# Attention scores by one plain fp32 product in place of three fp32r products of split parts

## The chip, the cores and the metric

The kernel runs on one core of a Trainium2 chip. Its engines are TensorE (PE; its weight loads are listed as PEld), VectorE (DVE), ScalarE (ACT), GpSimd (POOL) and SyncE (SP), which issues most DMAs. Each engine works through its own queue in order and waits on semaphores for the others. The metric is the device time of one execution in microseconds, as the median of several.

## The reference

Sliding-window attention with four sink keys, then two mixture-of-experts layers. The change concerns the scores alone:

```python
def _attn_ref(q, k, v, n_sink, window) -> np.ndarray:      # q, k, v: 4 x 8 x 768 x 64, fp32
    scale = 1.0 / np.sqrt(D)
    scores = scale * np.matmul(q, k.transpose(0, 1, 3, 2))
    is_sink = pos[None, :] < int(n_sink)                   # n_sink = 4
    in_window = (rel >= 0) & (rel < int(window))           # window = 128
    scores = np.where(is_sink | in_window, scores, -1000000000.0)
    scores = scores - np.max(scores, axis=-1, keepdims=True)
    a = np.exp(scores)
    a = a / (np.sum(a, axis=-1, keepdims=True) + 1e-09)
    return np.matmul(a, v).astype(np.float32)

def reference(**kwargs):
    x = attn_out.transpose(0, 2, 1, 3).reshape(B * S, H * D)
    x = _moe_ref(x=x, **moe_kwargs)      # one expert of 8 per token, by its logits and a bias per modality
    return _moe2_ref(x=x, **moe2_kwargs) # experts with a fixed capacity
```

## The kernel before

**Tiling.** The attention stage works on pairs of heads, 16 in all (4 batches of 4 pairs). The two heads of a pair lie on partitions 0 to 63 and 64 to 127 of `qr` and `kr`, transposed, so that the contraction is over 64 partitions. A pair has six query blocks of 128 rows. The loop runs over the 96 blocks; block i of a pair is scored against 260 columns: 128 keys of the block before, 4 sink keys and its own 128 keys (132 columns for the first block, which has no block before it).

**Order.** The stage is pipelined by hand: `ORDER` (line 174) lists what is issued in each turn of the loop, and each step works on a block some turns back. Per turn: the exponential of the block before (`ex`), loads (`ld`), the score product (`qk`), a piece of background work such as the router's bookkeeping for a finished batch (`bg`), the product with v of six blocks back (`pv`), mask and row maximum of this block (`mm`), transposes of P of two blocks back (`tr`, `se`); every second turn the output rows (`ro`, `oT`, `xo`) and the sink columns (`sp`, `st`, `so`). The scores `sp` have two buffers in PSUM, so block n waits until the exponential of block n-2 has read its own.

**Scores before.** Each load of q and k is split for the pair that follows: `split_hi` rounds to fp32r on ACT (`qh` is q times 0.125, `kh` is k), `split_lo` forms what the rounding left (`ql` on DVE; `kl` on POOL for three pairs in four and on DVE for the fourth), a third of a tile at a time, at six turns per pair. `qk_mm` adds three products for each head: qh kh, qh kl, ql kh. The two heads' products use different partitions and different PSUM banks.

**Sinks.** The four sink columns of P are packed with their own split parts in `psk` (`sinkpack`, POOL), transposed on PE against `identr`, an fp32r copy of the identity (`sinktr`), copied out by ACT, and used in `rows` together with the transposed output. The transposes of P itself (L359), the product with v (L388) and the second part of `rows` (L428) are plain fp32; the sink transposes (L405) and the first part of `rows` (L426) are fp32r.

**After the attention.** `moe1` and `moe2` compute the expert layers by split fp32r products. The ids, rows and weights of the first experts are fetched from within the attention's loop, on SP's and POOL's queues.

Of the kernel before, what the change touches and what calls it, by code (L numbers as in the profile page):

```python
# [10 lines left out]
F32 = mybir.dt.float32  # L11
F32R = mybir.dt.float32r
BF = mybir.dt.bfloat16
I32 = mybir.dt.int32
AF = mybir.ActivationFunctionType
OP = mybir.AluOpType
# [3 lines left out]
B, H, S, D = 4, 8, 768, 64  # L20
NB = S // 128
NP = H // 2
# [6 lines left out]
KW = NB * SEG  # L29
# [33 lines left out]
def bc(ap, shape):  # L63
    return ap.to_broadcast(shape)
# [7 lines left out]
def load_consts(nc, g, cpool, cst):  # L72
    g.cp = cpool
    g.cst = cpool.tile([128, C_W], F32, name="cst")
    g.ident = g.cst[:, C_ID:C_ID + 128]
    g.identr = cpool.tile([128, 128], F32R, name="identr")
    g.tri = cpool.tile([128, 128], BF, name="tri")
    g.ones = cpool.tile([128, 128], BF, name="ones")
    g.iota = g.cst[:, C_IOTA:C_IOTA + 128]
    g.wz = cpool.tile([128, 512], BF, name="wz")  # L80
    nc.gpsimd.memset(g.wz, 0.0)

    def derive():
        nc.vector.tensor_copy(g.identr, g.ident)
        nc.vector.tensor_copy(g.tri, g.cst[:, C_TRI:C_TRI + 128])
        nc.vector.memset(g.ones, 1.0)
    g.cst_load = lambda: nc.sync.dma_start(g.cst, cst)
    g.cst_derive = derive
# [82 lines left out]


LM, LE, LT, LP, LK, LS, LO, LR = 0, 1, 2, 6, 3, 6, 8, 9
ORDER = "ex ld qk ini bg pv mm tr ro oT sp st xo so lo hi se"


def attention(ctx, tc, g, qT, kT, v4, vsT, vsR, wg, put_x, after_batch, bg, drain=True):
    nc = tc.nc
    one = ctx.enter_context(tc.tile_pool(name="at1", bufs=1))
    wk = ctx.enter_context(tc.tile_pool(name="at2", bufs=2))  # L180
# [4 lines left out]
    raw, qk, vt = {}, {}, {}  # L185

    def load_pair(p):
        if p >= B * NP:
            return
        b, pr = divmod(p, NP)  # L190
        qr = wk.tile([128, S], F32, name="qr")
        kr = wk.tile([128, KW], F32, name="kr")
        nc.sync.dma_start(qr, qT[b, pr])
        nc.sync.dma_start(kr, kT[b, pr])
        raw[p] = (qr, kr)

    def split_hi(p, c):
        if p >= B * NP:
            return
        if c == 0:  # L200
            qk[p] = [wk.tile([128, S], F32R, name="qh"), wk.tile([128, S], F32R, name="ql"),
                     wk.tile([128, KW], F32R, name="kh"), wk.tile([128, KW], F32R, name="kl")]
        qr, kr = raw[p]
        qh, ql, kh, kl = qk[p]
        c2 = c % 3
        if c < 3:
            r = slice(256 * c2, 256 * c2 + 256)
            nc.scalar.activation(qh[:, r], qr[:, r], AF.Copy, scale=0.125)
        else:
            r = slice(264 * c2, 264 * c2 + 264)  # L210
            nc.scalar.activation(kh[:, r], kr[:, r], AF.Copy)

    def split_lo(p, c):
        if p >= B * NP:
            return
        qr, kr = raw[p]
        qh, ql, kh, kl = qk[p]
        c2 = c % 3
        if c < 3:
            r = slice(256 * c2, 256 * c2 + 256)  # L220
            nc.vector.scalar_tensor_tensor(ql[:, r], qr[:, r], 0.125, qh[:, r].bitcast(F32), op0=OP.mult,
                                           op1=OP.subtract)
        else:
            r = slice(264 * c2, 264 * c2 + 264)
            (nc.gpsimd if p % 4 < 3 else nc.vector).tensor_tensor(kl[:, r], kr[:, r], kh[:, r].bitcast(F32), op=OP.subtract)

    def load_v(p):
        if p < B * NP:
            vt[p] = wk.tile([128, NB, 2, D], F32, name="vr", bufs=3)
            nc.sync.dma_start(vt[p], v4[p // NP, p % NP])  # L230

    load_pair(0)
    g.cst_load()
    load_pair(1)
    load_v(0)

# [17 lines left out]
    for s in range(2):  # L254
        o = slice(64 * s, 64 * s + 64)
# [7 lines left out]
    nc.gpsimd.memset(bd.bitcast(F32), 0.0)  # L263
    vsh = wk.tile([96, B * NP, 72], F32, name="vsh", bufs=1)
    msk = one.tile([128, 3, 128], I32, name="msk")
    for c in (0, 3, 1, 4, 2, 5):
        split_hi(0, c)
    for c in (0, 3):
        split_lo(0, c)
    for i, c in ((1, C_M0), (2, C_M1), (0, C_CAUS)):  # L270
        nc.vector.tensor_copy(msk[:, i, :], g.cst[:, c:c + 128])

    def init(n):
        V = nc.vector
        if n < 2:
            for c in ((4, 1), (5, 2))[n]:
                split_lo(0, c)
        if n == 0:
            g.cst_derive()
            V.tensor_copy(rw[:, :, 0:128], bc(g.ident[:, None, :], [128, NP, 128]))  # L280
        if n in (2, 4):
            g.pw = ps.tile([96, B * NP, 8], F32, name="px")
        for p in {2: range(4), 4: range(4, 10), 5: range(10, 16)}.get(n, ()):
            nc.tensor.matmul(g.pw[:, p, :], vst[:, p, :], wgp[:, p % NP, :], start=True, stop=True)
        if n in (3, 6):
            r = slice(0, 4) if n == 3 else slice(4, 16)
            V.tensor_copy(vsx[:, r, 64:72], g.pw[:, r])
            V.tensor_copy(vsh[:, r].bitcast(F32R), vsx[:, r])
        if n in (4, 7):
            r = slice(0, 4) if n == 4 else slice(4, 16)  # L290
            V.tensor_tensor(vsh[64:96, r].bitcast(F32R), vsx[64:96, r], vsh[64:96, r], op=OP.subtract)
        k = n - 5 if n < 9 else (4 + (n - 9) // 2 if (n - 9) % 2 == 0 else 16)
        if 0 <= k < 16:
            c, m = divmod(k, 4)
            blk, hd = divmod(m, 2)
            mk = g.cst[:96, C_BD + m:C_BD + m + 1]
            r = slice(4 * c, 4 * c + 4)
            o, i = bd[:, r, blk, 64 * hd:64 * hd + 64], vsh[:, r, 0:64]
            if c > 0:
                nc.gpsimd.tensor_scalar(o, i, mk, None, op0=OP.mult)  # L300
            else:
                nc.scalar.activation(o, i, AF.Copy, scale=mk)
            V.tensor_scalar(bd[:, r, blk, 128 + 8 * hd:136 + 8 * hd], vsh[:, r, 64:72], mk, None, op0=OP.mult)

    st = {}

    def unit(n):
        p, i = divmod(n, NB)
        b, pr = divmod(p, NP)
        return b, pr, p, i  # L310

    def qk_mm(n):
        b, pr, p, i = unit(n)
        qh, ql, kh, kl = qk[p]
        sp = ps.tile([128, 2, 512], F32, name="sp", bufs=2)
        c0 = 128 if i == 0 else 0
        k0 = SEG * i - 128 + c0
        for j, (x, y) in enumerate(((qh, kh), (qh, kl), (ql, kh))):
            for hd in range(2):
                o = 64 * hd  # L320
                nc.tensor.matmul(sp[:, hd, c0:260], x[o:o + 64, 128 * i:128 * i + 128],
                                 y[o:o + 64, k0:k0 + 260 - c0], start=(j == 0), stop=(j == 2))
        st[n] = K()
        st[n].sp = sp

# [75 lines left out]
    def sinktr(gn, pt):  # L401
        s = st[2 * gn + 1]
        s.skp = (ps.tile([128, 512], F32, name="pt") if pt is None else pt)[0:96, 384:512]
        sk = psk[gn % 4]
        nc.tensor.transpose(s.skp.bitcast(F32R), sk.rearrange("p a b c -> p (a b c)"), g.identr)  # L405

    def sinkout(gn):
        s = st[2 * gn + 1]
# [47 lines left out]
    def at(n, lag, last=NU):  # L456
        return n - lag if lag <= n < last + lag else None

    def sink(n, lag):
        m = n - lag  # L460
        return m // 2 if 0 <= m and m % 2 == 0 and m // 2 < NU // 2 else None

    def when(f, *a):
        return lambda n: None if f(n) is None else a[0](f(n))

    def loads(n):
        b, pr, p, i = unit(n)
        if i == 1:
            load_pair(p + 2)
            load_v(p + 1)  # L470

    def one_of(n, f):
        p, i = divmod(n, NB)
        f(p + 1, i)

    ops = dict(
        ld=when(lambda n: at(n, 0), loads),
        qk=when(lambda n: at(n, 0), qk_mm),
        mm=when(lambda n: at(n, LM), mask_max),
        ex=when(lambda n: at(n, LE), exp),  # L480
        tr=when(lambda n: at(n, LT), trans),
        se=when(lambda n: at(n, LT), sel),
        st=when(lambda n: sink(n, LS), lambda k: sinktr(k, st[2 * k + LS - LT].ptt if 2 * k + LS - LT < NU else None)),
        so=when(lambda n: sink(n, LS), sinkout),
        sp=when(lambda n: sink(n, LK), sinkpack),
        oT=when(lambda n: sink(n, LO), outT),
        ro=when(lambda n: sink(n, LR), rows),
        xo=when(lambda n: sink(n, LR), xout),
        pv=when(lambda n: at(n, LP), pv),
        hi=when(lambda n: at(n, 0), lambda n: one_of(n, split_hi)),  # L490
        lo=when(lambda n: at(n, 1), lambda n: one_of(n, split_lo)),
        bg=lambda n: bg.pop(1),
        ini=init)
    for n in range(NU + LR + 3):
        for op in ORDER.split():
            if op == "qk" and n < 6:
# [1446 lines left out]
```

## Time and profile before

| what | value |
|---|---|
| three runs | 942.4, 949.34, 950.2 us (median 949.34) |
| the profiled execution | 948.23 us, span 946.4 us, mean granted clock 0.951 |
| PE busy over the span | 877.8 us (93%) |
| DVE, ACT, POOL busy | 668.4, 429.9, 386.3 us |
| attention stage, by the last of its output rows on PE | to 212 us |

The span is from the first to the last instruction; the execution's own time is 1.8 us longer. Busy shares over the span mix three stages, so the attention is read from its own stretches. Durations of matmuls overlap, so PE's busy time says less than the starts of its rows. The granted clock is TensorE's, as a share of 2.4 GHz; at any one time it is 1.00 or 0.50.

### The profile page before, as it was taken

The numbers are of one execution on the slowest core, as the hardware profiler recorded it, in microseconds if no ns is written. First come the engines' busy times: TensorE is split into PE (matmuls) and PEld (weight loads), VectorE is DVE, ScalarE is ACT, GpSimd is POOL, SyncE is SP. The second block draws the span as 40 slices with busy tenths as digits, with TensorE's granted clock in tenths as the row PEclk, the third lists the DMA queues.
The fourth block names the chain that finished last, engine by engine and source line by source line (L and its number), as shares of the span: only waits on it lengthen the run. The fifth ranks groups of instructions, "written<-read, shape, count | busy, mean of one in ns | idle before, by whom it ended". The sixth has DMA issues, their size and how long they took to land. (4 is left out here: it accounts for less than half of the span.)

```text
span 946.4 us, 15922 instructions
## 1 busy us (share of the span) xinstructions
PE 877.8 (93%) x5226; PEld 697.2 (74%) x5232; DVE 668.4 (71%) x1876; ACT 429.9 (45%) x1231; POOL 386.3 (41%) x636
## 2 busy tenths in 40 slices
PE   8998989998999999999998868889999998999993
PEld 4666767666888888888876635778788787798992
DVE  5999989867669697878863936878878677723210
ACT  4787968764343334343334503233334342345430
POOL 5897969783311010100000003645364554457441
PEclk9899999899999999999996877999999999999997
DMA  8344646366444444433434206234453433434200
GB/s 235 103 145 127 134 138 119 119 229 202 111 157 134 135 146 138 161 129 128 133 114 135 87 15 211 90 123 157 146 180 109 145 123 101 144 124 157 89 34 36
DMA packets 68952, 124.02 MB, mean 131 GB/s; under 512 B 9075, under 2 KB 21365, under 8 KB 68726
## 3 DMA queue, kind: packets, MB, share of 16 engines
q1 hardware_dynamic: 62166, 103.41, 35.3%
q0 software_dynamic: 6688, 19.43, 6.5%
q8 instruction: 46, 0.75, 0.3%
q14 instruction: 52, 0.43, 0.2%
HBM read 103.11 MB, written 19.71 MB: 130 GB/s over the span
## 5 line engine op out<-in xcount | busy, mean ns | idle before, releaser
L965 ACT ACTIVATE hh<-ph 128x384 fp32r<-128x384 f32 (+1 forms) x112 | 60.2, 538 | 272.3 <-PE ph L956 271.8
L956 PE MATMUL ph<-xh,w1h 128*128 128x384 f32 (+1 forms) x448 | 170.9, 382 | 0.0
L899 PE MATMUL y<-w2h,hh 128*128 128x512 f32 x400 | 163.5, 409 | 0.0
L956 PE MATMUL ph<-xh,w1l 128*128 128x384 f32 (+1 forms) x448 | 163.3, 364 | 0.0
L956 PE MATMUL ph<-xl,w1h 128*128 128x384 f32 (+1 forms) x448 | 161.9, 364 | 0.0
L899 PE MATMUL y<-w2h,hl 128*128 128x512 f32 x400 | 159.3, 398 | 0.0
L899 PE MATMUL y<-w2l,hh 128*128 128x512 f32 x400 | 159.0, 398 | 0.0
L966 DVE SCALAR_TENSOR_TENSOR hl<-ph,hh 128x384 fp32r<-128x384 f32 (+1 forms) x112 | 68.5, 611 | 110.2 <-ACT hh L965 109.7
L1111 POOL DMA_INDIRECT xg<-xd,ent x26 | 27.4, 1055 | 219.3 <-DMA ent<-idtab 169.4
L852 POOL TENSOR_TENSOR w2l<-w2r,w2h 128x512 fp32r<-128x512 f32 x64 | 87.7, 1374 | 52.5 <-ACT w2h L848 37.6
L1151 DVE SCALAR_TENSOR_TENSOR junk<-yr,wgb 128x512 f32<-128x512 f32 x160 | 103.3, 684 | 0.0
L956 PEld LDWEIGHTS ph<-xh,w1h 128*128 128x128 f32 x448 | 86.4, 193 | 10.4
L956 PEld LDWEIGHTS ph<-xh,w1l 128*128 128x128 f32 x448 | 86.2, 192 | 9.7
L956 PEld LDWEIGHTS ph<-xl,w1h 128*128 128x128 f32 x448 | 85.5, 191 | 7.8
L899 PEld LDWEIGHTS y<-w2h,hl 128*128 128x128 f32 x400 | 76.2, 191 | 17.1 <-DVE hl L1004 0.4
L899 PEld LDWEIGHTS y<-w2h,hh 128*128 128x128 f32 x400 | 76.6, 192 | 12.4 <-ACT hh L1003 0.4
L899 PEld LDWEIGHTS y<-w2l,hh 128*128 128x128 f32 x400 | 76.4, 191 | 12.2 <-DVE w2l L852 0.3
L871 DVE TENSOR_TENSOR w1l<-w1r,w1h 128x512 fp32r<-128x512 f32 x96 | 73.6, 767 | 13.5 <-ACT w1h L866 13.5
L866 ACT ACTIVATE w1h<-w1r 128x512 fp32r<-128x512 f32 x128 | 79.7, 623 | 5.7 <-DMA w1r<-in_w_dram 3.0
L351 ACT ACTIVATE P<-sp,mx 128x132 f32<-128x132 f32 x192 | 69.3, 368 | 28.4 <-DVE mx L340 27.7
L848 ACT ACTIVATE w2h<-w2r 128x512 fp32r<-128x512 f32 x128 | 79.4, 624 | 2.4 <-issue 2.0
L1596 POOL DMA_INDIRECT xg<-xs,idx x24 | 25.0, 1042 | 111.3 <-DMA w2r<-in_w_dram 90.6
(351 smaller groups left out, 1682.7 us busy)
## 6 DMA issues: line engine op xcount, KB each, us to landing
w1r<-in_w_dram SPq DMA_DIRECT2D x32, 1024.0 KB, 5.4
w2r<-in_w_dram SPq DMA_DIRECT2D x32, 1024.0 KB, 6.0
xs<-yr SPq DMA_DIRECT2D x26, 256.0 KB, 6.1
kr<-in_kT_dram SPq DMA_DIRECT2D x16, 396.0 KB, 3.5
qr<-in_qT_dram SPq DMA_DIRECT2D x16, 384.0 KB, 4.0
vr<-in_v_dram SPq DMA_DIRECT2D x16, 384.0 KB, 4.0
xd<-xb SPq DMA_DIRECT2D x16, 384.0 KB, 4.5
wgb<-in_wg2T_dram SPq DMA_DIRECT2D x1, 2048.0 KB
```

Of the source, the lines that this page charges most:

```text
L351: nc.scalar.activation(s.P[:, i % 2, hd, :], s.sp[:, hd, 128:260], AF.Exp, bias=s.mx[:, hd:hd + 1], accum_out=s.sm[:, i % 2, hd:hd + 1])
L848: nc.scalar.activation(ch[1][c][0], r[:, q, :], AF.Copy)
L852: eng.tensor_tensor(lo, r[:, q, :], h.bitcast(F32), op=OP.subtract)
L866: nc.scalar.activation(h, v, AF.Copy)
L871: eng.tensor_tensor(lo, v, h.bitcast(F32), op=OP.subtract)
L899: nc.tensor.matmul(o, l, r, start=(first and i == 0), stop=(end and i == 2))
L956: nc.tensor.matmul(ph, wp[:, c, :], xp_[:, c, 0:NTK], start=(d == 0 and i == 0), stop=(d == 3 and i == len(cut[d]) - 1))
L965: nc.scalar.activation(hh, ph, AF.Relu)
L966: nc.vector.scalar_tensor_tensor(hl, ph, 0.0, hh.bitcast(F32), op0=OP.max, op1=OP.subtract)
L1111: self.nc.gpsimd.indirect_dma_start(out=self.xg[j][:, a, :], out_offset=None, in_=self.G.xd[0:k, :], in_offset=bass.IndirectOffsetOnAxis(a ...
L1151: V.scalar_tensor_tensor(junk, yr[:, 0:DM], 1.0, wgb[:, e, :], op0=OP.mult, op1=OP.mult, accum_out=lg[:, e:e + 1])
L1596: self.nc.gpsimd.indirect_dma_start(out=xg[:, a, :], out_offset=None, in_=self.xs, in_offset=bass.IndirectOffsetOnAxis(ap=self.idx[k][:, 0 ...
```

## The change

The scores of each head come from one product in plain fp32, of the loaded k and of q times 0.125 (`qs`, made on ACT in three pieces per pair at every second block). `split_hi`, `split_lo` and their four tiles go; `kr` is read by the product itself and gets a third buffer. The sink transposes use the fp32 identity and read `psk` as plain fp32; `identr` goes.

```diff
@@ load_consts
-    g.identr = cpool.tile([128, 128], F32R, name="identr")
-        nc.vector.tensor_copy(g.identr, g.ident)
@@
-ORDER = "ex ld qk ini bg pv mm tr ro oT sp st xo so lo hi se"
+ORDER = "ex ld qk ini bg pv mm tr ro oT sp st xo so sq se"
@@ load_pair
-        kr = wk.tile([128, KW], F32, name="kr")
+        kr = wk.tile([128, KW], F32, name="kr", bufs=3)
@@
-    def split_hi(p, c):
...
-    def split_lo(p, c):
...
+    def scale_q(p, c):
+        if p >= B * NP or c % 2:
             return
         if c == 0:
+            qk[p] = wk.tile([128, S], F32, name="qs")
+        r = slice(128 * c, 128 * c + 256)
+        nc.scalar.activation(qk[p][:, r], raw[p][0][:, r], AF.Copy, scale=0.125)
@@ qk_mm
-        for j, (x, y) in enumerate(((qh, kh), (qh, kl), (ql, kh))):
-            for hd in range(2):
-                o = 64 * hd
-                nc.tensor.matmul(sp[:, hd, c0:260], x[o:o + 64, 128 * i:128 * i + 128],
-                                 y[o:o + 64, k0:k0 + 260 - c0], start=(j == 0), stop=(j == 2))
+        for hd in range(2):
+            o = 64 * hd
+            nc.tensor.matmul(sp[:, hd, c0:260], qs[o:o + 64, 128 * i:128 * i + 128], kr[o:o + 64, k0:k0 + 260 - c0],
+                             start=True, stop=True)
@@ sinktr
-        nc.tensor.transpose(s.skp.bitcast(F32R), sk.rearrange("p a b c -> p (a b c)"), g.identr)
+        nc.tensor.transpose(s.skp, sk.bitcast(F32).rearrange("p a b c -> p (a b c)"), g.ident)
```

On PE, in the steady part of the loop (the first two blocks of a pair) before:

```order
L321 MATMUL sp<-kh,qh 128x132 x2
L321 MATMUL sp<-kl,qh 128x132 x2
L321 MATMUL sp<-kh,ql 128x132 x2
L359 MATMUL pt<-cst,P 128x128 x2
L405 MATMUL pt<-identr,psk_177 96x128
L321 MATMUL sp<-kh,qh 128x260 x2
L321 MATMUL sp<-kl,qh 128x260 x2
L321 MATMUL sp<-kh,ql 128x260 x2
L388 MATMUL po<-lu,vr 64x256 x2
L359 MATMUL pt<-cst,P 128x128 x2
L426 MATMUL px<-bd,skT 128x288
L428 MATMUL px<-rw,oT 128x144 x2
```

The same place on PE after the change, where line 291 is `qk_mm` and 375 `sinktr`:

```order
L291 MATMUL sp<-kr,qs 128x132 x2
L329 MATMUL pt<-cst,P 128x128 x2
L375 MATMUL pt<-cst,psk_176 96x128
L291 MATMUL sp<-kr,qs 128x260 x2
L358 MATMUL po<-lu,vr 64x256 x2
L329 MATMUL pt<-cst,P 128x128 x2
L396 MATMUL px<-bd,skT 128x288
L398 MATMUL px<-rw,oT 128x144 x2
```

Six score products of a block became two; the operations around them stand as they stood.

On DVE, two blocks of a pair before (masks and maxima at L338 and L340, output rows at L442 to L448):

```order
L338 COPY_PREDICATED sp<-msk,sp 128x2x128
L340 TENSOR_REDUCE mx<-sp 128x2
L442 TENSOR_SCALAR rv<-sm 128x4
L443 RECIPROCAL rv<-rv 128x4
L445 TENSOR_TENSOR xb<-px,rv 128x256
L448 TENSOR_TENSOR lp<-px,rv 128x2x16
L221 SCALAR_TENSOR_TENSOR ql<-qr,qh 128x256
L338 COPY_PREDICATED sp<-msk,sp 128x2x128
L340 TENSOR_REDUCE mx<-sp 128x2
L225 TENSOR_TENSOR kl<-kr,kh 128x264
```

The same place on DVE after (the lines are 30 lower):

```order
L308 COPY_PREDICATED sp<-msk,sp 128x2x128
L310 TENSOR_REDUCE mx<-sp 128x2
L412 TENSOR_SCALAR rv<-sm 128x4
L413 RECIPROCAL rv<-rv 128x4
L415 TENSOR_TENSOR xb<-px,rv 128x256
L418 TENSOR_TENSOR lp<-px,rv 128x2x16
L308 COPY_PREDICATED sp<-msk,sp 128x2x128
L310 TENSOR_REDUCE mx<-sp 128x2
```

The splits between one block's maximum and the next block's mask are gone; nothing took their place.

## Rows read from the trace of the kernel before

**Rows 1.** Stretches: length; PE, PEld, DVE, ACT, POOL busy; granted clock; DMA share; GB/s.
```profile
203.80:212.40 8.60, 7.18 (x58) 4.84 (x56) 3.33 (x18) 2.95 (x11) 7.09 (x12) 1.00 1.01 367
100.00:112.50 12.50, 12.50 (x121) 8.93 (x119) 11.36 (x35) 11.20 (x50) 11.76 (x29) 1.00 0.64 129
162.50:175.00 12.50, 10.28 (x72) 7.26 (x72) 11.51 (x47) 7.53 (x33) 9.07 (x25) 0.73 0.59 188
```
**Rows 2.** Waits, 0 to 205 us: total us, times, longest.
```profile
ACT P L351 <- DVE mx L340: 27.7, 43, 2.8
PEld sp L321 <- ACT P L351: 17.9, 29, 2.4
```
**Rows 3.** PE's timeline, 101 to 108 us: start, us to the end, what.
```profile
101.07 0.30 PE L405 MATMUL pt<-identr,psk 128*96 128x128 f32 x1
101.33 0.39 PE L321 MATMUL sp<-kh,qh 64*128 64x260 f32 x2
101.56 0.28 PE L321 MATMUL sp<-kl,qh 64*128 64x260 f32 x2
101.67 0.28 PE L321 MATMUL sp<-kh,ql 64*128 64x260 f32 x2
101.89 0.65 PE L388 MATMUL po<-lu,vr 128*64 128x256 f32 x4
102.47 0.44 PE L359 MATMUL pt<-cst,P 128*128 128x128 f32 x2
...
102.88 0.65 PE L428 MATMUL px<-rw,oT 128*128 128x144 f32 x4
...
107.39 0.33 PE L321 MATMUL sp<-kh,qh 64*128 64x132 f32 x2
...
107.87 0.44 PE L359 MATMUL pt<-cst,P 128*128 128x128 f32 x2
```
**Rows 4.** PE's timeline: score products of first blocks of three pairs.
```profile
37.86 0.33 PE L321 MATMUL sp<-kh,qh 64*128 64x132 f32 x2
...
118.04 0.33 PE L321 MATMUL sp<-kh,qh 64*128 64x132 f32 x2
...
192.73 0.33 PE L321 MATMUL sp<-kh,qh 64*128 64x132 f32 x2
```
**Rows 5.** Groups by form, 0 to 205 us: count, busy us, mean ns, idle before.
```profile
L388 PE MATMUL po<-lu,vr 128*64 128x256 f32 x184 | 30.9, 415 | 0.0
L428 PE MATMUL px<-rw,oT 128*128 128x144 f32 x176 | 30.3, 296 | 0.0
L225 POOL TENSOR_TENSOR kl<-kr,kh 128x264 fp32r<-128x264 f32 x36 | 27.2, 757 | 0.2
...
L221 DVE SCALAR_TENSOR_TENSOR ql<-qr,qh 128x256 fp32r<-128x256 f32 x48 | 24.7, 516 | 4.7 <-ACT qh L208 4.7
...
L211 ACT ACTIVATE kh<-kr 128x264 fp32r<-128x264 f32 x48 | 20.1, 418 | 0.7 <-DMA kr<-in_kT_dram 0.7
...
L225 DVE TENSOR_TENSOR kl<-kr,kh 128x264 fp32r<-128x264 f32 x12 | 6.4, 534 | 0.0
```
**Rows 6.** The timeline of the loads on PE at 101 us, second pair.
```profile
101.44 0.19 PEld L321 LDWEIGHTS sp<-kl,qh 64*128 64x128 f32 x2
```
**Rows 7.** DVE's timeline around 165 us.
```profile
163.48 0.66 DVE L221 SCALAR_TENSOR_TENSOR ql<-qr,qh 128x256 fp32r<-128x256 f32 x1
...
166.71 0.41 DVE L338 COPY_PREDICATED sp<-msk,sp 128x256 f32<-128x256 int32 x1
```
**Rows 8.** PE's timeline, 168 to 174 us, with idle time before and its releaser.
```profile
168.49 0.48 PE L321 MATMUL sp<-kh,qh 64*128 64x132 f32 x2 [2.22 <-ACT P L351]
...
172.82 1.16 PE L428 MATMUL px<-rw,oT 128*128 128x144 f32 x4
```
**Rows 9.** PE's timeline in the first pair.
```profile
13.65 0.82 PE L284 MATMUL px<-wgp,vst 128*96 128x8 f32 x8 [0.66 <-DMA vst<-in_vsT_dram]
```

More of the change, by code (lines that the diff above doesn't have):

```diff
@@ L195, in load_pair @@
         raw[p] = (qr, kr)
-    def split_hi(p, c):
-        if p >= B * NP:
+    def scale_q(p, c):
+        if p >= B * NP or c % 2:
             return
         if c == 0:
[L201 to L211, printed above, removed]
-    def split_lo(p, c):
[L214 to L225, printed above, removed]
+            qk[p] = wk.tile([128, S], F32, name="qs")
+        r = slice(128 * c, 128 * c + 256)
+        nc.scalar.activation(qk[p][:, r], raw[p][0][:, r], AF.Copy, scale=0.125)
     def load_v(p):
@@ L265, in attention @@
     msk = one.tile([128, 3, 128], I32, name="msk")
[L266 to L269, printed above, removed]
+    for c in (0, 2, 4):
+        scale_q(0, c)
     for i, c in ((1, C_M0), (2, C_M1), (0, C_CAUS)):
@@ L274, in init @@
         V = nc.vector
-        if n < 2:
-            for c in ((4, 1), (5, 2))[n]:
-                split_lo(0, c)
         if n == 0:
@@ L313, in qk_mm @@
         b, pr, p, i = unit(n)
-        qh, ql, kh, kl = qk[p]
+        qs, kr = qk[p], raw[p][1]
         sp = ps.tile([128, 2, 512], F32, name="sp", bufs=2)
@@ L489, in attention @@
         pv=when(lambda n: at(n, LP), pv),
-        hi=when(lambda n: at(n, 0), lambda n: one_of(n, split_hi)),
-        lo=when(lambda n: at(n, 1), lambda n: one_of(n, split_lo)),
+        sq=when(lambda n: at(n, 0), lambda n: one_of(n, scale_q)),
         bg=lambda n: bg.pop(1),
```

## The prediction

> **What bounds the kernel now.** The change touches only the attention stage, the first 212 us of 946.4; what follows it is taken as it is. I read the busy time by stretch first [rows 1]. In a quiet stretch (100 to 112.5 us) PE is busy for 12.50 of 12.50 us, but DVE for 11.36, ACT for 11.20 and POOL for 11.76 as well, so four engines are nearly full together. In a bad stretch (162.5 to 175) PE falls to 10.28 and ACT to 7.53 while DVE keeps 11.51: there DVE sets the pace.
>
> Matmul durations overlap, so a PE that is busy all the time need not be the limit. The order of the starts decides. In a quiet pair (six query blocks of one pair of heads) the PE rows follow each other without a hole [rows 3], and the pair takes 118.04 - 107.39 = 10.65 us [rows 3, 4]. That is PE's floor for a pair. The 13 pairs from 37.86 to 192.73 us took 154.87 us [rows 4], 11.91 each; 13 floors are 138.5, so 16.4 us are excess.
>
> The waits say where the excess comes from [rows 2]: PE's score product waits for ACT's exponential (17.9 us at PE's loads in 29 waits), and the exponential for DVE's maximum (27.7 us in 43). Both scores buffers are then in use: the product of a block cannot start until the exponential of the block two before it has read its buffer. The worst case shows it [rows 7, 8]: from 163.48 to 166.71 us DVE does a split of q (0.66) and some bookkeeping of the router before it gets to the next mask, and PE stands for 2.22 us at 168.49. So the stage is PE's floor, plus what DVE's bursts cost on top.
>
> **What the change removes.** The splits: DVE loses 48 of q (24.7 us) and 12 of k (6.4 us), POOL 36 of k (27.2 us), ACT 48 roundings of k (20.1 us) [rows 5]. In the 13 pairs DVE loses 39/48 of 24.7 plus all 6.4, 26.5 us or 2.0 per pair. On PE 6 products per block become 2. None of these times comes off the end as such: in a quiet pair PE's own work hides them, and they only count where PE waits.
>
> **What it adds: the score product.** Before, a block of 260 columns holds PE from 101.33 to 101.89 us, 0.56 us [rows 3]: 0.11 until the second load may start [rows 6], then three products of two heads, the last two starting 0.11 apart (101.56, 101.67), which is 260 columns at one per cycle of 2.4 GHz. The last takes 0.22 to the next operation, 0.11 of streaming and 0.11 of changing over. Both heads run at once: each row of two records is no longer than one.
>
> No row shows a plain fp32 product on 64 of the 128 rows. The nearest are two. The plain fp32 product of L428 appears as twice as many records as the program has instructions, so each runs as two passes; four passes of 144 columns take 0.65 us from first start to last end, one lasts 0.296, so they start (0.65 - 0.30)/3 = 0.118 apart [rows 3, 5]. That is 0.82 ns a column, two cycles. And the plain product with v (L388), two heads on two halves of the columns: four passes of 256 columns from 101.89 take 0.65 in all, while one lasts 0.415 [rows 3, 5]. One after the other they would take 3 x 0.21 + 0.42 = 1.05. So the two heads' passes run side by side there.
>
> I price the new product like that: 0.11 for the first load, two passes of 260 x 0.82 = 0.21, and 0.11 to change over, 0.65 us against 0.56: **+0.09 per block**. The second load hides under the first pass. For the first block of a pair (132 columns) three products take 0.48 (107.39 to 107.87) [rows 3] and are held by their loads; the new one takes 0.11 + 2 x 0.108 + 0.11 = 0.43: -0.05. The ends of the price are 0.43 (two passes and no overhead) and 1.07 (four passes one after the other, 0.11 + 4 x 0.213 + 0.11); I stay with 0.65, since the L388 row shows the same instruction on two heads.
>
> The Trainium skill speaks against the change here: "FP8 and Floating Point Precision", section TensorE Precision Notes, counts true fp32 as four passes through the array. By that the product goes from three column times to four, an estimate of +0.108 per block in place of +0.09, and the trace agrees with it: two records at two cycles a column. With it the sum below would be 1.2 us higher.
>
> **The sink transposes.** The fp32r one streams 128 columns and stands 0.26 us before the next product (101.07 to 101.33) [rows 3]. Plain, I give it two cycles a column: 128 x 0.41 ns = +0.05 each, three per pair. Ends: 0 and +0.11. The identity's copy on DVE disappears, once.
>
> **PE's floor after.** 10.65 + 5 x 0.09 - 0.05 + 3 x 0.05 = **11.20 us a pair**. The floor rises, because PE is the one engine that gets more work.
>
> **What is left of the excess.** DVE's 2.0 us less and PE's 0.55 more give DVE some 2.5 us of slack per pair, where there was next to none. Single splits then no longer reach PE; the bursts of bookkeeping still do in part. In the 163 us case, 0.57 of the 3.2 us of delay was the split; the rest remains, less what DVE is now ahead, so perhaps 1 us of the 2.2. I take a quarter of 16.4, **4 us**, ends 0 and 10.
>
> **Queues.** ACT's scaling of q stands where the rounding stood; three of six places per pair are empty. On SP the loads of k now wait for PE's last product of the pair before, where they waited for ACT and for POOL or DVE; with a third buffer that is over five blocks before the load is issued, so nothing queues behind it. The loads that follow in the queue (v, x out, the first experts' weights) are issued at the same block as before. Cost 0; if a k load stood, v's load and the write of x would stand behind it, and the PE would wait at the first block of a pair.
>
> **Head and tail.** The first two pairs (7.55 to 37.86) are held by masks, waits for loads and warm-up matmuls; for instance PE stands 0.66 us for vst at 13.65 [rows 9], which remains. Twelve DVE splits leave there, of which I count 1 us in the end after PE's +0.09 per block (ends +1 and -4). The last pair and its drain add 0.5: its six products and sink transposes, with no excess to give back.
>
> **The sum.** 13 x 11.20 + 4 = 149.6 against 154.9: -5.3; head -1; tail +0.5: **-5.8 us**. The profiled execution took 948.23 us (span 946.4, 1.8 around it), 1.1 below the median of the three runs. 948.2 - 5.8 = 942.4; I say **942.5**. One per cent is 9.5 us, which is about what a measurement of this kernel can tell from no change (its own three runs lie between 942.4 and 950.2).
>
> **Rivals.**
> *The heads do not pair up (slower).* On 64 rows the passes of the two heads run one after the other. Against: the fp32r products pair up on rows, and plain ones on columns [rows 3]. For: no row shows both together. Price: +0.51 per block, +0.17 per first block, a pair of 13.5 us; 13 x 13.5 = 175.5, +20.6 with no excess left, +2.3 in the last pair, +4 in the head: **975**. It decides as soon as a block's product holds PE for more than about 0.75 us, since then PE's floor passes 11.9 - 0.3. The skill's "TensorEngine Tiling (Array Packing)", Key Properties, says that tiles work independently, which is for pairing; no run here shows it for this operation.
>
> *The clock falls (slower).* At the lower level L428's four passes take 1.16 us for 0.65 [rows 3, 8], 1.8 times. The quiet stretch and the tail from 203.8 to 212.4, which is mostly plain fp32 work with PE at 7.18 of 8.60 us, were granted 1.00 [rows 1]; the fall at 168 came after a stop of 2.2 us. So PE should be granted the full clock at least as often. A quarter of the 13 pairs at the lower level would cost 36 x 0.8 = 29: **971**. Eight more us at that level take the gain away.
>
> *The excess is not DVE's.* If bursts, and not splits, make all of the 16.4 us, 13 x 11.20 + 16.4 = 162: +7.1 and +0.5, less 1 of the head: **955**, PE's longer products with nothing in return.
>
> *All of it goes (faster).* With POOL and ACT lighter too, the excess vanishes and the head gives 4: 145.6 - 154.9 - 4 + 0.5 = -12.8: **935.5**.
>
> **How the numbers follow.** Forecast 0.58 (spread 937 to 951 by the ends of 4 us of excess and of the head), all of it goes 0.18, excess not DVE's 0.10, heads in turn 0.09, clock 0.05. The range 934 to 958 takes in the first three, 0.86. Faster by over 1% (under 938.7): the 0.18 and some 0.05 of the forecast, 0.23. Slower by over 1%: the 0.14 and 0.02 of the third, 0.16. Within: 0.61.
>
> **What would show it.** A quiet pair of 11.2 us, by the starts of the first blocks' products; a block's product of 0.65 us to the next PE operation, its two passes 0.32 apart, each with two records at one time; DVE under 10 us busy per 12.5 us; the wait of the exponential for the maximum well below 27.7 us; POOL waiting more. I am wrong if the records of the two heads start apart, if quiet pairs still take 10.7, or if the 13 pairs keep their excess with DVE idle.

## The result, and the profile after

The kernel after takes **937.22 us** (median of 9 runs, 932.86 to 940.63) against 948.75 for the kernel before beside it (9 runs, 942.40 to 952.48): ratio **0.9877, 95% interval 0.9858 to 0.9895**. The gain is real and over one per cent. The forecast, 942.5 with a range of 934 to 958, had the direction and held the time, but it gave only 0.6% and lay nearer to no change than the result does.

The profiled execution took 933.44 us (span 931.6), 14.8 below that of before. Its stages, by the same landmarks in both traces:

| stage | before, us | after, us | difference |
|---|---|---|---|
| start to the first block of the third pair | 37.86 | 34.82 | -3.0 |
| the 13 pairs after it | 154.87 | 146.84 | -8.0 |
| last pair and drain, to the first transpose of the expert layers | 19.93 | 20.55 | +0.6 |
| attention in all | 212.66 | 202.21 | -10.45 |
| expert layers and the rest (code unchanged) | 733.7 | 729.4 | -4.3 |

The busy time by stretch of the kernel after; columns as in [rows 1]. The first stretch is the whole of the 13 pairs:

```profile
34.82:181.66 146.84, 145.92 (x1123) 90.62 (x1122) 117.81 (x420) 117.83 (x510) 102.34 (x302) 1.00 0.52 139
...
193.40:202.00 8.60, 7.17 (x56) 4.74 (x56) 3.17 (x17) 2.85 (x10) 7.05 (x12) 1.00 1.05 385
100.00:112.50 12.50, 12.50 (x101) 7.68 (x97) 9.21 (x28) 10.36 (x46) 8.58 (x26) 1.00 0.63 129
```

Against the quiet stretch of [rows 1], PE is still busy throughout (12.50), while DVE went from 11.36 to 9.21, ACT from 11.20 to 10.36 and POOL from 11.76 to 8.58. For the 13 pairs the trace of before has these rows: first all of them, then two single pairs:

```profile
37.86:192.73 154.87, 145.58 (x1280) 102.79 (x1280) 141.23 (x469) 125.82 (x549) 127.56 (x326) 0.97 0.49 129
...
131.47:144.64 13.17, 12.70 (x100) 8.92 (x101) 11.88 (x46) 9.90 (x44) 7.74 (x24) 0.87 0.45 104
168.49:182.07 13.58, 13.58 (x99) 9.65 (x99) 11.33 (x41) 10.39 (x45) 7.56 (x23) 0.75 0.29 89
```

DVE gave back 23.4 us in these pairs and POOL 25.2. The granted clock is the second thing to see: 0.97 before, with 0.87 and 0.75 in two of its longest pairs, and 1.00 after. So a part of the old excess may be TensorE's own time at the lower level; the section on the prediction works out how much.

The waits of the kernel after, 0 to 195 us, answer to [rows 2]:

```profile
POOL lu L337 <- ACT t L335: 59.8, 55, 7.7
...
DVE sp L308 <- PE sp L291: 14.9, 30, 0.8
...
ACT P L321 <- DVE mx L310: 8.6, 18, 1.4
```

The exponential's wait for the maximum fell from 27.7 us in 43 to 8.6 in 18, and a new one stands above it: DVE's mask now waits for PE's product, 14.9 us, where it waited 2.0 us before. The direction of waiting has turned: in the 13 pairs PE is busy for 145.92 of 146.84 us, and it is the bound.

PE's own rows in a quiet pair, which answer to [rows 3], and two first blocks, which answer to [rows 4]:

```profile
102.08 0.50 PE L291 MATMUL sp<-kr,qs 64*128 64x132 f32 x4
102.51 0.44 PE L329 MATMUL pt<-cst,P 128*128 128x128 f32 x2
102.78 0.27 PE L375 MATMUL pt<-cst,psk 128*96 128x128 f32 x1
102.98 0.71 PE L291 MATMUL sp<-kr,qs 64*128 64x260 f32 x4
103.62 0.65 PE L358 MATMUL po<-lu,vr 128*64 128x256 f32 x4
...
113.27 0.49 PE L291 MATMUL sp<-kr,qs 64*128 64x132 f32 x4
...
181.66 0.49 PE L291 MATMUL sp<-kr,qs 64*128 64x132 f32 x4
```

Four records a block are two heads of two passes. The block's product holds PE from 102.98 to 103.62, 0.64 us, and the first block's from 102.08 to 102.51, 0.43. The block's two passes start 0.32 us apart, as forecast. This quiet pair takes 113.27 - 102.08 = 11.19 us, the shortest takes 11.17. The 13 pairs hold 146.84 - 13 x 11.17 = 1.6 us over 13 of the shortest, where before they held 16.4.

### The profile page after: what moved, and what is told of

It reads as the page before. It is cut to its first block, busy times and chain, and to the rows that moved or that the text cites. A ratio compares the mean times of both kernels' runs of the same rounds, so it can differ in the third digit from the quotient of the medians.

```text
span 931.6 us, 15380 instructions
## 1 busy us (share of the span) xinstructions
PE 877.2 (94%) x5034; PEld 680.8 (73%) x5040; DVE 637.6 (68%) x1815; ACT 419.8 (45%) x1183; POOL 354.4 (38%) x600
## 5 line engine op out<-in xcount | busy, mean ns | idle before, releaser
L840 POOL TENSOR_TENSOR w1l<-w1r,w1h 128x512 fp32r<-128x512 f32 x32 | 43.8, 1369 | 62.7 <-ACT w1h L835 62.7
```

The source lines that it names most:

```text
L840: eng.tensor_tensor(lo, v, h.bitcast(F32), op=OP.subtract)
```

## The experiments

Each pair time below runs between the first score products of two pairs; "13 pairs" is from the third to the sixteenth. A stage time is from one profiled execution, a ratio from the timed runs beside the kernel before. "The splits" are the 48 of q on DVE, 12 and 36 of k on DVE and POOL, and 48 roundings of k on ACT. The forecasts below call the run with all splits e1 and the one with DVE's e2.

| kernel | 13 pairs, us | quiet pair | attention, us | ratio of the whole, 95% interval |
|---|---|---|---|---|
| before | 154.87 | 10.65 | 212.66 | 1 |
| after | 146.84 | 11.17 | 202.21 | 0.9877 [0.9858, 0.9895] |
| after, profiled again | 146.86 | 11.18 | 202.31 | 0.9882 [0.9825, 0.9940] |
| after + all splits (e1) | 156.40 | 11.17 | 213.41 | 1.0053 [1.0025, 1.0081] |
| after + DVE's splits (e2) | 149.61 | 11.17 | 205.83 | 0.9971 [0.9938, 1.0005] |
| after + ACT's and POOL's | 153.02 | 11.17 | 209.29 | 0.9972 [0.9939, 1.0004] |
| after + POOL's | 148.05 | 11.17 | 204.35 | 0.9903 [0.9867, 0.9939] |
| after + ACT's | 146.84 | 11.17 | 202.49 | 0.9866 [0.9817, 0.9915] |
| before without low parts | 142.47 | 10.67 | 197.53 | 0.9894 [0.9840, 0.9947] |

### Relief or product: all splits kept, and relief alone

The first kernel is the kernel after, with every split still computed, at its old place, into tiles that no product reads:

```diff
+    def dead_hi(p, c):
...
+        if c >= 3 and True:
...
+            nc.scalar.activation(dd[p][1][:, r], raw[p][1][:, r], AF.Copy)
...
+    def dead_lo(p, c):
...
+            if True:
+                nc.vector.scalar_tensor_tensor(ql[:, r], qr[:, r], 0.125, qr[:, r], op0=OP.mult, op1=OP.subtract)
...
+            x = kh[:, r].bitcast(F32) if True else kr[:, r]
+            if p % 4 < 3 and True:
+                nc.gpsimd.tensor_tensor(kl[:, r], kr[:, r], x, op=OP.subtract)
+            if p % 4 == 3 and True:
+                nc.vector.tensor_tensor(kl[:, r], kr[:, r], x, op=OP.subtract)
...
```

> The plain fp32 product, with all of the old splits still computed and not used (ACT 48, DVE 60, POOL 36; the split of q subtracts q itself). Theory A, the gain is relief from the splits: quiet pairs keep PE's new floor of 11.2 us, but the excess comes back, the 13 pairs take 152 to 158 us instead of 146.8, the whole 944 to 952 us. Theory B, the gain is the product itself (fewer matmuls and waits on PE): the 13 pairs stay at 147 to 149 us, the whole at 936 to 940.

Measured: 952.02 us, ratio 1.0053 [1.0025, 1.0081]. The 13 pairs take 156.40 us, as theory A has it. With the splits back the whole gain is gone and a little more; the new product by itself is a small loss.

The second kernel is the kernel before without low parts: its three fp32r products stay, on rounded parts, and the splits of DVE and POOL go. ACT's 48 roundings of k stay, which the kernel after has not.

```diff
-        for j, (x, y) in enumerate(((qh, kh), (qh, kl), (ql, kh))):
+        for j, (x, y) in enumerate(((qh, kh), (qh, kh), (qh, kh))):
...
-    def split_lo(p, c):
...
```

> The kernel before with the second parts of the split left out: three fp32r products of the rounded parts (q scaled by 0.125/3), no subtraction on DVE or POOL; the scores lose the low bits. PE's work is that of before, and DVE's and POOL's splits are gone. If DVE's splits made the excess: quiet pairs at 10.65 us, the 13 pairs 139 to 142 us, the whole 926 to 932 us. If the excess is not theirs: the 13 pairs above 150 us. The difference to the changed kernel is then the price of the plain product and transposes, 13 x 0.53 = 7 us.

Measured: 935.38 us, ratio 0.9894 [0.9840, 0.9947], 13 pairs 142.47 us: nearly all of the excess goes, but both numbers are a little over what was forecast. The relief gives more in this stage than the whole change does: with the new product and its floor the 13 pairs are 4.4 us longer. That is less than the floor's rise, 13 x (11.17 - 10.67) = 6.5: 3.8 us of excess are left here, 1.6 in the kernel after. That the longer product gives DVE time would explain it; no run isolates that. The whole does not tell the two kernels apart (0.9894 and 0.9877).

### Whose splits: DVE's alone, ACT's and POOL's, POOL's alone, ACT's alone

My reasons named DVE. These four keep one part of the splits each. The edit is the one above with a part switched off, for instance for POOL alone:

```diff
-        if c >= 3 and True:
+        if c >= 3 and False:
...
-            if True:
+            if False:
...
-            x = kh[:, r].bitcast(F32) if True else kr[:, r]
+            x = kh[:, r].bitcast(F32) if False else kr[:, r]
...
-            if p % 4 == 3 and True:
+            if p % 4 == 3 and False:
```

With ACT's roundings off, the subtraction takes k from k: it no longer depends on ACT, and it reads one tile instead of two.

> As e1, but only DVE's splits are kept (48 of q, 12 of k). If the relief was DVE's (theory A as predicted): the 13 pairs take 150 to 156 us, most of what e1 loses, and the head loses 1 to 2 us. If it was ACT's and POOL's relief that counted: within 2 us of 146.8.

> As e1, but only ACT's roundings of k (48) and POOL's splits of k (36) are kept. If the relief was DVE's: the 13 pairs take 147 to 149 us and the head is within 1 us of the changed kernel's. If ACT and POOL counted: 150 to 156 us, and e2 stays near 147.

Measured over the 146.84 us of the kernel after: DVE's splits +2.8 us, ACT's and POOL's together +6.2, all +9.6. Put on top of the other half, each costs a little more: DVE's 156.40 - 153.02 = 3.4, ACT's and POOL's 156.40 - 149.61 = 6.8. The ratios of the whole are alike (0.9971 and 0.9972), since the unchanged rest took 737.4 us in the one profile and 732.7 in the other; only the stage tells the halves apart. There DVE's splits are the smaller part, and that falsifies the attribution in my prediction.

> The kernel after with only GpSimd's 36 subtractions of k still computed (into a tile nobody reads; the part of k subtracted is k itself). The 13 quiet-to-quiet pairs (pair 2 to pair 14) took 146.8 us in the kernel after and 153.0 us with ScalarE's 48 and GpSimd's 36 splits kept. GpSimd theory (its extra 0.74 us pieces leave no pause between its instructions, and VectorE instructions with two SBUF inputs are held until it pauses, 2.75 us twice in that trace): here 151 to 153 us, with one or more VectorE instructions over 1.5 us. ScalarE theory (its 0.42 us roundings delay the exponentials): here 147 to 148.5 us and no VectorE instruction over 1 us. Total 941 to 945 by the first, 936 to 939 by the second.

> The kernel after with only ScalarE's 48 roundings of k still computed (into a tile nobody reads). ScalarE theory: the 13 pairs take 151 to 153 us against 146.8 in the kernel after, total 941 to 945. GpSimd theory: 147 to 148.5 us, total 936 to 939, and the waits of the exponentials for VectorE's maximum stay near the 6 us of the kernel after.

Measured: POOL's alone +1.2 us (ratio 0.9903), ACT's alone +0.0 (0.9866). Neither theory gets its number: each alone costs little, both together 6.2. But POOL's part alone is lighter than its part in the pair of them: the subtraction of k from itself takes 0.62 us, that of the rounded k 0.74 (median of 29 in the 13 pairs). Memsets of 0.74 us in its place cost 2.5 (below). So DVE's part adds to the others almost in full, and ACT's and POOL's cost more together than the sum of what was measured alone; how much of that is the heavier subtraction was not isolated.

### Held instructions: a memset in POOL's place, the held instruction moved, and once more

An instruction is called held here when it takes several times its usual length while GpSimd works. The trace of the kernel with ACT's and POOL's splits shows two such, in two of its longer pairs. These are DVE's and then POOL's timeline near 60 us, in the second run of the same kernel:

```profile
59.09 0.43 DVE L347 TENSOR_REDUCE mx<-sp 128x2 f32<-128x264 f32 x1
59.44 2.77 DVE L311 TENSOR_SCALAR bd<-vsh,cst 96x32 fp32r<-96x32 f32 x1
62.12 0.41 DVE L341 COPY_PREDICATED sp<-msk,sp 128x256 f32<-128x256 int32 x1
```
```profile
59.26 0.74 POOL L229 TENSOR_TENSOR kl<-kr,kh 128x264 fp32r<-128x264 f32 x1
59.95 0.41 POOL L374 TENSOR_SCALAR_AFFINE_SELECT lu<-t 128x256 f32<-128x256 f32 x1
60.31 0.41 POOL L377 TENSOR_SCALAR_AFFINE_SELECT lu<-t 128x256 f32<-128x256 f32 x1
60.69 0.74 POOL L229 TENSOR_TENSOR kl<-kr,kh 128x264 fp32r<-128x264 f32 x1
61.38 0.40 POOL L374 TENSOR_SCALAR_AFFINE_SELECT lu<-t 128x256 f32<-128x256 f32 x1
61.74 0.41 POOL L377 TENSOR_SCALAR_AFFINE_SELECT lu<-t 128x256 f32<-128x256 f32 x1
62.13 0.93 POOL L308 TENSOR_SCALAR bd<-vsh,cst 96x256 fp32r<-96x256 f32 x1
```

A DVE instruction of 32 columns takes 2.77 us, where it takes 0.25 when free. It starts 0.18 us into a subtraction on POOL and ends when POOL's sixth instruction does; POOL does not pause in between. The mask behind it waits, and then PE does too, for 1.22 us:

```profile
64.12 0.71 PE L328 MATMUL sp<-kr,qs 64*128 64x260 f32 x4 [1.22 <-ACT P L358]
```

This pair takes 12.46 us. The next has the same hold near 72 us and the same stop of 1.22 us, and takes 13.26. The kernel before has one too, in the pair of 13.43 us that begins at 118.04 [rows 4] (DVE's timeline of before):

```profile
120.19 2.07 DVE L335 COPY_PREDICATED sp<-msk,neg 128x8 f32<-128x8 int32 x1
122.30 0.43 DVE L340 TENSOR_REDUCE mx<-sp 128x2 f32<-128x264 f32 x1
```

The Trainium skill has the rule: "SBUF — State Buffer", section Who interferes with whom, says that GpSimd shares a port pair with VectorE as an exclusive lock, that a VectorE instruction in a two-port mode contends for it, that one with two SBUF inputs does so against a GpSimd instruction that reads SBUF but not against one that only writes it, and that the later one blocks until the other is through. The trace agrees that the instruction is held, but here it is held through six GpSimd instructions, not one.

**A memset in place of the subtraction** writes SBUF and reads nothing.

```diff
-                nc.gpsimd.tensor_tensor(kl[:, r], kr[:, r], x, op=OP.subtract)
+                nc.gpsimd.memset(kl[:, 0:768].bitcast(F32), 0.0)
```

> As the run with GpSimd's 36 subtractions kept, with each subtraction replaced by a memset of 128x768 fp32 (about 0.7 us by the 1.81 us that a memset of 2048 columns takes), which writes SBUF and reads nothing. If what costs is that VectorE instructions are held while GpSimd reads SBUF, they get through during a memset: no VectorE instruction over 1 us, and the 13 pairs take 147 to 149.5 us. If what costs is only that GpSimd's own work behind it (the weights' triangle cuts) comes late, or that GpSimd writes too, this is as long as the run with subtractions, within 1 us.

Measured: 13 pairs 149.38 us, 1.3 more than with subtractions, ratio 0.9904 [0.9867, 0.9941]. The memsets are longer than those subtractions (0.74 us for 0.62). The time is at the top of what the reading theory gave, and its reason holds for one kind of instruction and falls for another. It falls for the addition of a constant in these rows of DVE and POOL, which has one tile as input.

```profile
152.39 0.77 DVE L449 TENSOR_SCALAR rv<-sm 128x4 f32<-128x4 f32 x1
```
```profile
152.37 0.76 POOL L229 MEMSET kl<- 128x768 f32 x1
153.07 0.42 POOL L374 TENSOR_SCALAR_AFFINE_SELECT lu<-t 128x256 f32<-128x256 f32 x1
```

Four columns take 0.77 us, where they take 0.17 when free, to the end of the memset. One such instruction took 1.15 us, to the end of the memset behind the one in which it began. So for this kind a GpSimd operation that only writes is no better. The masked copy of 8 columns, which reads two tiles in SBUF and was held in the kernel before, gets through a memset unhindered, here and again at 71.21:

```profile
60.03 0.17 DVE L342 COPY_PREDICATED sp<-msk,neg 128x8 f32<-128x8 int32 x1
```
```profile
59.93 0.73 POOL L229 MEMSET kl<- 128x768 f32 x1
```

**The held instruction moved to ACT**, in the kernel with ACT's and POOL's splits:

```diff
-            V.tensor_scalar(bd[:, r, blk, 128 + 8 * hd:136 + 8 * hd], vsh[:, r, 64:72], mk, None, op0=OP.mult)
+            o, i = bd[:, r, blk, 128 + 8 * hd:136 + 8 * hd], vsh[:, r, 64:72]
+            if c > 0:
+                nc.scalar.activation(o, i, AF.Copy, scale=mk)
+            else:
+                V.tensor_scalar(o, i, mk, None, op0=OP.mult)
```

> The kernel with ScalarE's 48 and GpSimd's 36 splits kept (13 pairs 153.0 us, against 148.1 with GpSimd's alone and 146.8 with ScalarE's alone), with 12 of the 16 small VectorE instructions that fill the weight blocks of the low part (96x32, 0.25 us when free) computed by ScalarE instead; two of them were held on VectorE for 2.75 us behind six GpSimd instructions without a pause. If such holds make the two kinds of splits cost more together than the sum of each alone (6.2 against 1.2 us), the 13 pairs come down to 148.5 to 150 us. If it is general crowding, the work only moves to an engine that is fuller, and they stay at 152 to 154 us.

> The same kernel as the run with ScalarE's 48 and GpSimd's 36 splits kept, once more on the chip that runs its variant. If the long holds belong to the order of the instructions, VectorE instructions of over 2 us stand at the same places (some 59.5 and 72 us) and the 13 pairs take 152 to 154 us; if they are an accident of one execution, they are elsewhere or gone and the pairs take 148 to 150 us.

Measured: 152.62 us with the instruction moved, 152.98 without, ratios 0.9983 [0.9949, 1.0016] and 0.9967 [0.9933, 1.0001]. The repeat has the two holds at the same places (59.44 and 71.90 us, both 2.77) and the same 13 pairs within 0.04 us, so they belong to the order of the instructions. By its number the run with the instruction moved speaks for crowding. Its DVE timeline shows that the edit did not take the hold away:

```profile
61.57 1.82 DVE L346 COPY_PREDICATED sp<-msk,neg 128x8 f32<-128x8 int32 x1
63.43 0.43 DVE L351 TENSOR_REDUCE mx<-sp 128x2 f32<-128x264 f32 x1
```

Now the next instruction that can be held, a masked copy of 8 columns, stands for 1.82 us. The two holds are 0.95 us shorter each, and their pairs 0.56 shorter each (11.90 and 12.70); other pairs took back 0.8 of that 1.1. PE's stop behind each hold is 0.49 us now instead of 1.22. The two pairs hold (12.46 - 11.17) + (13.26 - 11.17) = 3.4 of the 6.2 us; the stops right behind the holds are 2 x 1.22 = 2.4 of them, and 0.56 is another stop in the second pair. The rest of the 6.2 lies in four other pairs, in which DVE also does the router's bookkeeping. Holds are not all of it: with all splits kept only one of over 2 us is left (72.65 us), and the stage is the longest of the kernels after with splits kept.

Why POOL's splits escape when they are alone can be read at the same place of that kernel's trace, DVE first and then POOL:

```profile
59.81 0.23 DVE L311 TENSOR_SCALAR bd<-vsh,cst 96x32 fp32r<-96x32 f32 x1
```
```profile
59.10 0.80 POOL L229 TENSOR_TENSOR kl<-kr 128x264 fp32r<-128x264 f32 x1
59.86 0.45 POOL L374 TENSOR_SCALAR_AFFINE_SELECT lu<-t 128x256 f32<-128x256 f32 x1
```

POOL works there without a pause as well. The DVE instruction comes 0.71 us into the subtraction, near its end, gets in at once, and POOL's next one is a little longer for it (0.45 for 0.40). With ACT's roundings it comes 0.18 us into it and is passed over. So a few tenths of a microsecond in the phase of the two engines may decide the price. That the phase makes the difference between the two kernels is argued from these rows, not isolated: the subtraction is also shorter here (0.62 us where nothing delays it) and no longer depends on ACT.

### The price of the product when the heads do not pair up

```diff
-            o = 64 * hd
+            o = 0
```

> The kernel after with the score products of both heads on partitions 0 to 63 (head 1's scores are left out; head 0's are computed twice). If the two heads' fp32 passes run side by side only because they use different row halves, a block's four passes now stand one after another, about 1.07 us for 260 columns against 0.65, a quiet pair takes 11.18 + 5 x 0.43 + 0.22 = 13.5 us, and the 13 pairs some 175 to 180 us. If they go one after another anyway or the row halves don't matter, a quiet pair stays at 11.2 us.

Measured: 985.53 us (one run), 13 pairs 176.49 us at a granted clock of 1.00, quiet pair 13.55. A block on PE:

```profile
101.84 1.14 PE L291 MATMUL sp<-kr,qs 64*128 64x260 f32 x4
102.91 0.20 PE L577 MATMUL px<-oh,tri 128*128 128x48 bf16 x1
```

It holds PE for 1.07 us against 0.64. In the kernel after the records of the two heads start 6 to 7 ns apart; here they start 0.22 us apart. Here it is the row halves that let the fp32 passes run side by side.

### A version with the sink transposes back in fp32r

```diff
+    g.identr = cpool.tile([128, 128], F32R, name="identr")
...
+        nc.vector.tensor_copy(g.identr, g.ident)
...
-        nc.tensor.transpose(s.skp, sk.bitcast(F32).rearrange("p a b c -> p (a b c)"), g.ident)
+        nc.tensor.transpose(s.skp.bitcast(F32R), sk.rearrange("p a b c -> p (a b c)"), g.identr)
```

> The kernel after with the 48 sink transposes back in fp32r and the product in plain fp32. If a plain fp32 transpose of these 96 columns costs 0.05 us more on TensorE, a quiet pair is 11.18 - 0.15 = 11.03 us and the 13 pairs 144.9 against 146.8 us: 2 to 2.5 us less than the kernel after in all, beside it on this chip, about 0.25%. If the time is hidden, a quiet pair stays at 11.18 and the total does not move.

> The kernel after unchanged, on the chip that runs its variant with the sink transposes in fp32r: ratio to the kernel before 0.986 to 0.990, quiet pair 11.18 us, 13 pairs 146.8 within 1 us. The rest of the program after the attention stage, whose code is the kernel before's, shows by how much its time differs between executions: 729.4 us in the first profile against 733.7 in that of the kernel before.

```profile
101.11 0.30 PE L377 MATMUL pt<-identr,psk 128*96 128x128 f32 x1
101.34 0.71 PE L293 MATMUL sp<-kr,qs 64*128 64x260 f32 x4
```

Measured: quiet pair 11.03 us (three times 0.05 less), 13 pairs 144.98 against 146.86, attention 199.19 against 202.31. The term is confirmed. The total does not show it: 936.61 us, ratio 0.9876 [0.9827, 0.9924], against 936.33 and 0.9882. In its profiled execution the unchanged rest took 738.4 us, against 729.5. So it is the shorter attention stage in these two profiles, and not a shown gain.

## Why the prediction was right, and where its sizes were off

**PE's floor: right.** Predicted 11.20 us a pair, measured 11.17 to 11.19. The product was priced at 0.65 us and took 0.64, the first block's at 0.43 and took 0.43, the sink transpose at +0.05 and gave back 0.05 when undone. The block took 0.56 before, so it rose by 0.08 us; the other estimate beside it, +0.108, was farther off. The choice of the nearest row (plain fp32 on column halves) decided this; the run on one row half shows that the other end of the price, 1.07, was the true cost without pairing.

**What is removed counts only where PE waits: right.** All splits back, and the gain is gone. The product alone is no gain. But it was applied to DVE's splits only.

**"So the stage is PE's floor, plus what DVE's bursts cost on top": the step that failed.** I put all 16.4 us of excess on DVE. Beside the 1.6 us that stay, three things were in it.
- DVE's splits, 2.8 us alone on the kernel after, 3.4 on top of the others.
- ACT's and POOL's splits, 6.2 us there and 6.8 on top of DVE's. Of the 6.2, at most 3.4 are pairs in which POOL holds DVE. In [rows 7] I read 0.66 us for a split of q as its length; the mean of them is 0.52 [rows 5], and POOL worked without a pause beside it. I had POOL's 27.2 us as hidden, since the page shows no wait for it: a hold is inside the held instruction's busy time.
- The clock. The two pairs granted 0.87 and 0.75 spent 26% of 13.17 and 50% of 13.58 us at the lower level, 10.2 us in all. By L428's 0.65 and 1.16 us [rows 3, 8] these cost at most 10.2 x (1 - 0.65/1.16) = 4.5 us. In the second of these pairs PE does not stop after its first product, so the 13.58 - 10.65 = 2.9 us of excess there are the clock's: 6.8 us at that level, by the same ratio, make 3.0. In all kernels with the new product, and in the one of relief alone, the 13 pairs were granted 1.00. No run isolates the clock, but the run with all splits kept agrees with it:

```profile
36.48:192.88 156.40, 147.88 (x1123) 90.61 (x1122) 141.38 (x469) 126.37 (x550) 127.90 (x327) 1.00 0.50 129
```

DVE is as busy as before (141.4 us for 141.2), and PE stands idle for 156.40 - 147.88 = 8.5 us, before for 154.87 - 145.58 = 9.3. Yet the excess is 156.40 - 13 x 11.17 = 11.2 us and not 16.4; 16.4 less 4.5 is 11.9. The time that the longer product gives DVE may be in the difference too.

**The excess left: mis-sized.** Predicted 4 us (0 to 10), measured 1.6. A quarter of the excess was carried over on the view that only DVE's load falls.

**The head: mis-sized.** Predicted -1, measured -3.0, within its ends. Part of it is the same kind of hold: the three casts that make the masks took 2.03 us before and 0.50 after, and beside them POOL ran a subtraction of k and three memsets without a pause only before. In every run with POOL's work kept the casts took 1.55 to 2.63 us, in every one without it 0.50 to 1.01. Another part may be the clock, granted 0.86 in the head before and 0.90 after.

**The tail: right**, +0.6 for +0.5.

**The sum.** Attention was to give 5.8 and gave 10.45, between the forecast and the rival in which all of the excess goes (12.8); the median, 937.22, is nearer that rival's 935.5, which had a chance of 0.18. The range held because its terms had wide ends: what the excess and the head give back was put too small by some 2 us each, and the two errors have the same sign. The rest of the program, in which I forecast no change, adds 4.3 us in the two profiles but hardly more than 1 by the medians (948.75 - 937.22 = 11.5, of which the stage gives 10.45): the profiled execution of the kernel after lies 3.8 us under its median. Two rivals are answered: the heads pair up, which the run on one row half shows for this operation, and the clock rose instead of falling. The third, that the excess is not DVE's, was half right in its cause and wrong in its price: the other engines' load went as well.

**What stays open.** The rest of the program, whose code is the same, took 729.4 to 738.4 us over the profiled kernels. In the two kernels that were profiled twice it repeats to 0.1 us (729.4 and 729.5; 732.7 and 732.8), but the nine timed runs of the kernel after lie 7.8 us apart. Of the 4.3 us here, 2.7 lie in one place near the middle of the program, between the same two products, in these stretches of before and then after:

```profile
528.90:556.00 27.10, 19.87 (x96) 14.15 (x98) 15.42 (x49) 10.67 (x19) 0.00 (x0) 0.94 0.19 62
```
```profile
518.40:542.80 24.40, 19.76 (x97) 14.03 (x97) 15.26 (x49) 10.68 (x19) 0.00 (x0) 0.98 0.19 67
```

The work is the same, the granted clock is 0.94 and 0.98, and PE's stop before the product that ends the stretch is 5.51 us before and 2.94 after. That stop is 2.6 of the 2.7 us; why it differs was not tried.

## What to carry to other kernels

Price a new TensorE operation from the row that shares its form, and work out the floor per period first: that part came out to 0.03 us a pair. For what other engines' relief gives, do not credit the engine that the waits name; remove each engine's work by itself and then together, and keep each part's instructions as long as they were: here the waits named DVE, whose splits were 2.8 of 9.6 us, and the lighter subtraction leaves POOL's own share open. A VectorE instruction that is now and then several times longer than its group's median, with GpSimd busy throughout, is a wait that the lists of waits of these traces do not show.

## What the runs showed of the hardware that was not expected

- A VectorE instruction that is held by GpSimd can be passed over by one GpSimd instruction after another: 2.77 us through six, at the same two places in two executions, and 1.82 us for another instruction when the first was moved. When it arrived 0.71 us into a 0.80 us operation, it got in at its end.
- A GpSimd memset, which reads no SBUF, held a VectorE addition of a constant to 4 columns for its whole 0.76 us, and let a masked copy of 8 columns with two SBUF inputs through in its usual 0.17.
- Two fp32 products of 64 rows each, on different row halves, run side by side: 0.64 us a block against 1.07 on the same half.
